# Two blocks' transposes moved from TensorE to DMA, and the visits of the second batch moved, in a sigmoid-attention and ReGLU kernel on Trainium2

## The chip, the cores and the metric

The kernel runs on one core of one Trainium2 chip. The metric is the device time of one execution in microseconds. Before the change it is 430.22 us, the median of three runs (430.01 to 430.52). The profile is of one execution, with a span of 428.4 us from the first instruction to the last.

## The reference

Sigmoid attention over 8 batches of 12 heads, 448 positions, 64 features a head, and then a ReGLU feed-forward layer on the 3584 tokens of 768 features, with a hidden width of 1536:

```python
scores = (1/sqrt(64)) * q @ k^T - log(448)
attn   = 1 / (1 + exp(-scores))
x      = (attn @ v), heads side by side            # 3584 x 768
out    = (max(x @ w_gate, 0) * (x @ w_val)) @ w_out
```

Inputs and output are in float32; the kernel multiplies in float16.

## The kernel before

The twelve heads of a batch form three blocks of four heads; block `n` has `b, i = divmod(n, 3)`, so that blocks 0 to 2 are batch 0, blocks 3 to 5 are batch 1, block 6 begins batch 2. A block has seven passes (chunks of 64 keys). Blocks 0 to 2 are worked off in a prologue. Then the loop over batches runs the feed-forward layer of batch `b` on TensorE and slips the attention of batch `b + 1` into it, in "visits" of three passes.

q and k must stand transposed, with the features on the partitions, before scores can be formed. There are two ways to that in the kernel. From block 6 on it is a DMA transpose on the SyncE queue; up to block 5 it is TensorE, with a copy out of PSUM:

```python
    def dma_transposes(n: int):
        for nm in ("k", "q"):
            h16 = qk16.pop((nm, n))
            t2 = qkTp.tile([P, NCH, 2, KC], FP16, tag="qkT", name=f"{nm}T")
            nc.sync.dma_start_transpose(
                t2[:].rearrange("p c h k -> p c (h k)"), h16[:].rearrange("p c r d -> p (c r d)")
            )
            qkT[nm, n] = t2

    def transposes(n: int, nm: str, *engines, cut=(0, NCH)):
        h16 = qk16.pop((nm, n))
        if n <= NBLK:
            tr = wkp.tile([P, NCH, 2, KC], FP16, tag="wk", name="tr")
        else:
            tr = qkp.tile([P, 2, 512], FP32, tag="qk", name="tr")[:, 0, 0 : S].bitcast(FP16)
            ...
        for c in range(cut[0], cut[-1]):
            nc.tensor.transpose(tr[:, c], h16[:, c, :, :], ident[:])
        ...                                   # one VectorE copy of tr into the qkT tile
```

The buffers that play a part: four tiles `qkT` (k and q of two blocks), four tiles `h16` (the float16 k and q before they are transposed), five staging tiles for weights, ten for q, k and v. PSUM has three tiles of two banks for scores, values and such (`qkp`) and two of one bank for the feed-forward layer (`wkp`).

A visit works off three passes; one of the two batch-1 blocks before may get its values (28 matmuls) in it. Each pass then calls `feed`:

```python
    def feed(i: int):
        n, c = divmod(i, NCH)
        m = n + 1
        if c == 0 and NPRO <= m < NB:          # NPRO is 6
            cast_block(m)
        if c == 4 and NBLK < m < NPRO:         # blocks 4 and 5
            later.append(m)
        if c == 3 and NPRO <= m < NB:
            dma_transposes(m)
        if c == 3 and NPRO <= m + 1 < NB:
            load_all(m + 1)
```

Weights and the inputs of blocks 3 to 5 are loaded in one order, one item at a time: ten items during the prologue, then one at every eighth step of the feed-forward layer. Each load is followed by its casts to float16 on GpSimd:

```python
        order = halves("g", 0) + ["kq"] + halves("u", 0) + ["v"] + halves("g", 1) + halves("u", 1)
        order += [4] + halves("g", 2) + halves("u", 2) + halves("o", 0) + [5]
        order += halves("o", 1) + halves("o", 2)

        def start_next():
            what = order.pop(0)
            if isinstance(what, int):
                load_all(what)                 # k, q, v of the block
                cast_block(what)               # q, k, v, on GpSimd
            ...
            else:
                load_w(*what)
                cast_w(*what, nc.gpsimd)
```

The loop, where a step is one matmul of a gate or value tile, or one of the down part:

```python
        for b in range(B):
            total = ffn_us(b)
            todo = []
            if b + 1 < B:
                count = NBLK * NCH // 3 + (1 if b == 0 else 0)
                lo = 6.0 if b == 0 else 0.0
                todo = [lo + (k + 0.5) * (total - lo) / count for k in range(count)]
            t = 0.0
            for step, cost in enumerate(ffn(b)):
                t += cost
                if order and step % 8 == 0:
                    start_next()
                if todo and t >= todo[0]:
                    due = todo.pop(0) + 2.0
                    visit()
                if later and t >= due:
                    m = later.pop(0)
                    transposes(m, "k")
                    transposes(m, "q")
```

`ffn(b)` takes the twelve gate and value tiles first (six matmuls for the gate, six for the value; the first pair of batch 0 is partly done before the loop) and then the down part with `wo`, in two column ranges of twelve matmuls for each 128 tokens. `total` is 38.88 in the kernel's own units for batch 0.

Of the kernel before, what the change touches and what calls it, by code (L numbers as in the profile page):

```python
# [16 lines left out]
def kernel(  # L17
# [16 lines left out]
    NBLK = H // HB  # L34
# [50 lines left out]
    def load_block(n: int, *which):  # L85
        b, i = divmod(n, NBLK)
        for nm, src, c0, c1, eng in which:
            st = stp.tile([P, 2, S], FP32, tag="st", name=f"st_{nm}")
            rows = src[b, i * HB : (i + 1) * HB].rearrange("(r h) (p c) d -> (h p) r (c d)", h=2, c=NCH)
            eng.dma_start(st[:, :, c0 * D : c1 * D], rows[:, :, c0 * D : c1 * D])  # L90
            staged[nm, n] = st

    def load_all(n: int, names="kqv"):
        for nm, src in (("k", k), ("q", q), ("v", v)):
            if nm in names:
                load_block(n, (nm, src, 0, NCH, nc.sync))

    def cast_qk(n: int, nm: str, *engines, cut=(0, NCH)):
        st = staged.pop((nm, n))
        h16 = h16p.tile([P, NCH, 2, D], FP16, tag="h16", name=f"h16{nm}")  # L100
        for c0, c1, eng in zip(cut, cut[1:], engines):
            o = h16[:, c0:c1].rearrange("p c r d -> p r c d")
            i = st[:, :, c0 * D : c1 * D].rearrange("p r (c d) -> p r c d", d=D)
            if eng is nc.scalar:
                eng.copy(o, i)
            else:
                eng.tensor_copy(o, i)  # L107
        qk16[nm, n] = h16

    def cast_v(n: int, eng):  # L110

        st = staged.pop(("v", n))
        t = v16p.tile([P, 2, S], FP16, tag="v16", name="v16")
        eng.tensor_copy(t[:, 0], st[:, 0])  # L114
        eng.tensor_copy(t[0:64, 1], st[64:128, 1])  # L115
        eng.tensor_copy(t[64:128, 1], st[0:64, 1])  # L116
        v16[n] = t

    def load_w(kind: str, j: int, half: int):

        st = swp.tile([P, WH], FP32, tag="sw", name=f"st_w{kind}")
        if kind == "o":
            r0 = (j * FG + half * FG // 2) * P
            src = moe_w_out[r0 : r0 + FG // 2 * P, :].rearrange("(c p) m -> p c m", p=P)
            nc.sync.dma_start(st[:].rearrange("p (c m) -> p c m", m=DM), src)
        else:
            w, r0 = moe_w_gate if kind == "g" else moe_w_val, half * NDC // 2 * P
            src = w[r0 : r0 + NDC // 2 * P, j * FG * P : (j + 1) * FG * P]
            nc.sync.dma_start(
                st[:].rearrange("p (c f) -> p c f", f=FG * P), src.rearrange("(c p) f -> p c f", p=P)  # L130
            )
        staged[kind, j, half] = st

    def cast_w(kind: str, j: int, half: int, eng):
        st = staged.pop((kind, j, half))
        dst = {"g": wg, "u": wv, "o": wo}[kind][j]
        n = (FG if kind == "o" else NDC) // 2
        dst = dst[:, half * n : (half + 1) * n].rearrange("p c f -> p (c f)")
        eng.tensor_copy(dst, st[:])  # L139
# [10 lines that stand above are left out]
# [165 lines left out]
    NPRO = 2 * NBLK  # L315

    def cast_block(n: int):
        cast_qk(n, "q", nc.gpsimd)
        cast_qk(n, "k", nc.gpsimd)
        cast_v(n, nc.gpsimd)  # L320

    def feed(i: int):

        n, c = divmod(i, NCH)
        m = n + 1
        if c == 0 and NPRO <= m < NB:
            cast_block(m)
        if c == 4 and NBLK < m < NPRO:
            later.append(m)
        if c == 3 and NPRO <= m < NB:  # L330
            dma_transposes(m)
        if c == 3 and NPRO <= m + 1 < NB:
            load_all(m + 1)
# [25 lines left out]
    def filler(*widths):  # L359

        if 0 not in PT:
            PT[0] = qkp.tile([P, 2, 512], FP32, tag="qk", name="pv_ps")
        for w in widths:
            nc.tensor.matmul(PT[0][:, 0, 0:w], zeros[:, 0:P], zeros[:, 0:w], start=True, stop=True)

    with tc.manual_schedule():
        nc.scalar.activation(warm[:], bias_t[:], AF.Sigmoid)  # L367

        sp, act = nc.sync, nc.scalar
        load_block(0, ("q", q, 0, NCH, sp), ("k", k, 0, 4, act), ("k2", k, 4, NCH, sp), ("v", v, 0, NCH, act))  # L370
        load_block(1, ("k", k, 0, NCH, sp), ("q", q, 0, NCH, act), ("v", v, 0, NCH, sp))
        load_block(2, ("k", k, 0, NCH, act), ("q", q, 0, NCH, sp), ("v", v, 0, NCH, sp))

        def halves(kind, j):
            return [(kind, j, 0), (kind, j, 1)]

        order = halves("g", 0) + ["kq"] + halves("u", 0) + ["v"] + halves("g", 1) + halves("u", 1)
        order += [4] + halves("g", 2) + halves("u", 2) + halves("o", 0) + [5]
        order += halves("o", 1) + halves("o", 2)

        def start_next():
            what = order.pop(0)
            if isinstance(what, int):
                load_all(what)
                cast_block(what)
            elif isinstance(what, str):
                load_all(NBLK, what)
                if what == "v":
                    cast_v(NBLK, nc.gpsimd)
# [4 lines that stand above are left out]
        filler(*[512] * 10)  # L394
        cast_qk(0, "q", nc.vector, nc.scalar, cut=(0, 4, NCH))
        cast_qk(0, "k", nc.vector, nc.scalar, cut=(0, 2, 4))
        transposes(0, "q")
        filler(128, 128)
        transposes(0, "k", nc.scalar, nc.vector, cut=(0, 2, 4))
        filler(128, 128, 128)  # L400
        cast_qk(0, "k2", nc.vector, cut=(4, NCH))
        for n in range(NBLK):
            cast_v(n, nc.gpsimd)
        for _ in range(2):
            start_next()


        NP0 = NBLK * NCH
        done = 0
        for i in range(NP0 + 2):  # L410
            n, c = divmod(i, NCH)
            if n < NBLK:
                scores(n, c)
            while done <= i - (4 if i < NP0 - 4 else 2):
                values(done // NCH, [done % NCH])
                done += 1
            if i == 2:
                qk16["k", 0] = qk16.pop(("k2", 0))
                transposes(0, "k", nc.vector, cut=(4, NCH))
            if 1 <= i <= 3:  # L420
                filler(256)
            if c == 1 and n + 1 < NBLK:
                cast_qk(n + 1, "k", nc.vector)
                cast_qk(n + 1, "q", nc.vector)
            if c in (3, 5) and n + 1 < NBLK:
                transposes(n + 1, "k" if c == 3 else "q")
            if i == 15:
                cast_qk(NBLK, "k", nc.vector)
            if i == 17:
                cast_qk(NBLK, "q", nc.vector)  # L430
                transposes(NBLK, "k")
            if i in (18, 21):
                gv_part(0, 0, wg, [0, 1] if i == 18 else [2, 3])
            if i == 20:
                transposes(NBLK, "q")
            if 11 <= i < NP0:
# [4 lines that stand above are left out]
            todo = []  # L441
            if b + 1 < B:
                count = NBLK * NCH // 3 + (1 if b == 0 else 0)
                lo = 6.0 if b == 0 else 0.0
                todo = [lo + (k + 0.5) * (total - lo) / count for k in range(count)]
            t = 0.0
            for step, cost in enumerate(ffn(b)):
# [10 lines that stand above are left out]
            for _ in todo:  # L458
                visit()
# [29 lines left out]
```

## Time and profile before

| | before |
|---|---|
| median time | 430.22 us |
| span of the profiled execution | 428.4 us |
| TensorE busy | 418.1 us, 98% |
| ScalarE, VectorE, GpSimd busy | 178.5, 166.5, 102.2 us |
| moved by DMA | 66.96 MB, 156 GB/s on average |
| TensorE transposes (`tr`) in the whole run | 84, of which 28 are blocks 4 and 5 |
| DMA transposes in the whole run | 36 |

In the page and the answers of the trace, a row names the line of the program, the engine, the operation, what it writes and what it reads. `gv_ps` are the gate and value tiles, `y_ps` the down part, `qk_ps` the scores, `pv_ps` the values, `tr` the TensorE transposes; `st_q`, `st_wo` and the like are staging tiles for loads, `h16k` and the like their float16 copies. PE is TensorE, DVE VectorE, ACT ScalarE, POOL GpSimd, SP SyncE. In a timeline or in the chain, the first number is the start in microseconds from the start of the span, the second the length; in brackets stands how long the engine sat idle before, and what ended that.

### The profile page before, as it was taken

To read this page: it belongs to the slowest core of one execution; us is meant where nothing else is said; L and a number is where in the kernel's file an instruction comes from. 1 tells how busy PE (TensorE), PEld (TensorE's weight loads), DVE (VectorE), ACT (ScalarE), POOL (GpSimd) and SP (SyncE) were. 2 spreads that over 40 slices of the span, in tenths; PEclk is the share of its full clock that TensorE was granted. 3 is DMA by queue.
4 is the path that set the end of the run, shared out by engine and by line. 5 is a ranking of instruction groups with operands and counts; after the bars stand their busy time and mean duration, and the time that the engine had idled before them with its cause. 6 is when DMAs were issued, how large, how long until landed. Compare 5 with 4: busy or idle time off the path is not lost.

```text
span 428.4 us, 7873 instructions
## 1 busy us (share of the span) xinstructions
PE 418.1 (98%) x3282; PEld 216.5 (51%) x3282; DVE 166.5 (39%) x276; ACT 178.5 (42%) x217; POOL 102.2 (24%) x137
## 2 busy tenths in 40 slices
PE   7789999999999999999999999999999999999996
PEld 4334555544555445545455444554455544555553
DVE  3555542353323452244423444244422435235531
ACT  5952566525434445444343545443435363500000
POOL 2567683333300333013120233003330030000000
PEclk9999999999999999999999999999999999999999
DMA  8999996673535753386623666247443730030014
GB/s 303 384 385 385 390 373 155 184 196 115 160 98 103 205 149 113 78 206 174 170 50 94 179 173 173 73 95 207 121 150 98 181 72 0 20 93 0 2 37 110
DMA packets 64371, 66.96 MB, mean 156 GB/s; under 512 B 35792, under 2 KB 54608, under 8 KB 64336
## 3 DMA queue, kind: packets, MB, share of 16 engines
q1 hardware_dynamic: 63088, 64.63, 51.8%
q10 hardware_dynamic: 1248, 1.84, 1.2%
q8 instruction: 25, 0.41, 0.4%
q14 instruction: 10, 0.08, 0.1%
HBM read 47.19 MB, written 11.01 MB: 136 GB/s over the span
## 4 chain that ended last, share of the span: by engine, by line
PE 93%; ACT 3%; DMA 2%; DVE 1%; issue 0%; ACTq 0%; DVEq 0%
PE gv_ps L232 51%; PE y_ps L275 26%; PE qk_ps L173 8%; PE pv_ps L197 7%; ACT PT L183 3%; DMA st_q<-in_q_dram 2%; PE tr L159 1%; DVE ysb L289 0%; DVE gate_sb L249 0%; DVE xT L213 0%; DVE h16q L107 0%; ACT L367 0%; ACT xT L211 0%; ACTq L295 0%; ACTq L90 0%
## 5 line engine op out<-in xcount | busy, mean ns | idle before, releaser
L183 ACT ACTIVATE PT<-qk_ps,bias_t 128x896 f16<-128x896 f32 x168 | 159.2, 1008 | 191.1 <-PE qk_ps L173 191.1
L232 PE MATMUL gv_ps<-xT,wg 128*128 128x448 f16 x576 | 128.1, 353 | 0.4 <-ACT xT L211 0.2
L232 PE MATMUL gv_ps<-xT,wv 128*128 128x448 f16 x576 | 126.9, 353 | 0.0
L275 PE MATMUL y_ps<-wo,hT 128*128 128x512 f16 (+2 forms) x684 | 113.7, 323 | 0.0
L275 PEld LDWEIGHTS <-hT 128*128 128x128 f16 x684 | 64.6, 98 | 48.0 <-issue 6.3
L249 DVE TENSOR_SCALAR gate_sb<-gv_ps 128x448 f32<-128x448 f32 x96 | 59.9, 624 | 73.4 <-PE gv_ps L232 73.4
L256 DVE TENSOR_TENSOR hT<-gate_sb,gv_ps 128x448 f16<-128x448 f32 x96 | 59.6, 621 | 64.3 <-PE gv_ps L232 64.2
L232 PEld LDWEIGHTS <-wg 128*128 128x128 f16 x576 | 55.0, 98 | 55.7 <-issue 7.7
L232 PEld LDWEIGHTS <-wv 128*128 128x128 f16 x576 | 55.0, 98 | 54.8 <-issue 5.2
L289 DVE TENSOR_SCALAR ysb<-y_ps 128x512 f32<-128x512 f32 (+2 forms) x56 | 31.1, 555 | 105.3 <-PE y_ps L275 104.1
L107 POOL CAST h16q<-st_q 128x896 f16<-128x896 f32 x20 | 18.6, 930 | 220.0 <-DMA st_q<-in_q_dram 195.3
L173 PE MATMUL qk_ps<-qT,kT 64*64 64x448 f16 x672 | 48.6, 358 | 3.9 <-ACT PT L183 2.9
L197 PE MATMUL pv_ps<-PT,v 64*64 64x448 f16 x672 | 39.1, 350 | 0.8 <-ACT PT L183 0.7
L173 PEld LDWEIGHTS <-kT 64*64 64x64 f16 x672 | 16.5, 105 | 29.8 <-issue 22.7
L197 PEld LDWEIGHTS <-v 64*64 64x64 f16 x672 | 19.9, 107 | 12.7 <-issue 2.1
L211 ACT ACTIVATE xT<-pv_ps 128x448 f16<-128x448 f32 x43 | 21.0, 547 | 6.0 <-PE pv_ps L197 4.8
L287 ACT ACTIVATE ysb<-y_ps 128x128 f32<-128x128 f32 x1 | 0.3, 277 | 44.8 <-PE y_ps L275 44.8
L107 POOL CAST h16k<-st_k 128x896 f16<-128x896 f32 x20 | 18.6, 928 | 0.0
L114 POOL CAST v<-st_v 128x448 f16<-128x448 f32 x24 | 13.3, 556 | 10.3 <-DMA st_v<-in_v_dram 10.3
L115 POOL CAST v<-st_v 64x448 f16<-64x448 f32 x24 | 13.4, 558 | 1.5
L116 POOL CAST v<-st_v 64x448 f16<-64x448 f32 x24 | 13.3, 555 | 1.0
L139 POOL CAST wv<-st_wu 128x1536 f16<-128x1536 f32 x6 | 8.8, 1467 | 5.7 <-DMA st_wu<-in_moe_w_val_dram 5.7
(26 smaller groups left out, 59.3 us busy)
## 6 DMA issues: line engine op xcount, KB each, us to landing
out_dram<-ysb SPq DMA_DIRECT2D x54, 192.0 KB, 2.7
st_q<-in_q_dram SPq DMA_DIRECT2D x23, 448.0 KB, 4.5
st_v<-in_v_dram SPq DMA_DIRECT2D x23, 448.0 KB, 5.2
st_k<-in_k_dram SPq DMA_DIRECT2D x22, 448.0 KB, 4.0
st_wg<-in_moe_w_gate_dram SPq DMA_DIRECT2D x6, 768.0 KB, 12.3
st_wu<-in_moe_w_val_dram SPq DMA_DIRECT2D x6, 768.0 KB, 12.2
st_wo<-in_moe_w_out_dram SPq DMA_DIRECT2D x6, 768.0 KB, 12.1
st_v<-in_v_dram ACTq DMA_DIRECT2D x1, 448.0 KB, 5.8
```

What stands on the lines that cost most here:

```text
L107: eng.tensor_copy(o, i)
L114: eng.tensor_copy(t[:, 0], st[:, 0])
L115: eng.tensor_copy(t[0:64, 1], st[64:128, 1])
L173: nc.tensor.matmul(ps[o : o + 64, bank, 0:S], kT[r : r + 64, c, h, :], qT[r : r + 64, :, h, :], start=True, stop=True, tile_position=(r, o ...
L183: nc.scalar.activation(pt[:], ps[:, :, 0:S], AF.Sigmoid, bias=bias_t[:], scale=qk_scale)
L197: nc.tensor.matmul(pv[o : o + 64, pr, 0:S], t[r : r + 64, pr, c * D : (c + 1) * D], pt[r : r + 64, pr, :], start=(c == 0), stop=(c == NCH ...
L211: nc.scalar.activation(x[:], pv[:, pr, 0:S], AF.Copy, scale=XSCALE)
L232: nc.tensor.matmul(begun[key][:, 0:S], w[j][:, dc, jj * P : (jj + 1) * P], xT[b, dc][:], start=(dc == 0), stop=(dc == NDC - 1),)
L249: nc.vector.tensor_scalar(out=g_sb[:], in0=gate[:, 0:S], scalar1=0.0, scalar2=None, op0=AOP.max)
L256: nc.vector.tensor_tensor(out=hT[f][:, o : o + S], in0=g_sb[:], in1=val[:, 0:S], op=AOP.mult)
L275: nc.tensor.matmul(y[:, 0:w], hT[f][:, o : o + P], wo[f // FG][:, f % FG, c0 : c0 + w], start=(f == 0), stop=(f == NFC - 1),)
L289: nc.vector.tensor_scalar(out=dst, in0=y[:, 0:w], scalar1=OUT_SCALE, scalar2=None, op0=AOP.mult)
```

## The change

Blocks 4 and 5 no longer go through TensorE. Their transposes are put into the load order as items of their own, `-4` behind the last gate and value weights and `-5` behind the last `wo`, and go to the SyncE queue as DMA transposes. The visits of batch 1 begin later in the feed-forward layer of batch 0 (`lo` is 10 in place of 6) and stand closer together, so that the transposes have time to come. The purpose is to free TensorE of 28 transposes and VectorE of four copies. The PSUM split and the matmuls on zeros ahead of the first tiles are as they were.

```diff
@@ feed
-        if c == 4 and NBLK < m < NPRO:
-            later.append(m)
@@ the load order
-        order += [4] + halves("g", 2) + halves("u", 2) + halves("o", 0) + [5]
-        order += halves("o", 1) + halves("o", 2)
+        order += [4] + halves("g", 2) + halves("u", 2) + [-4] + halves("o", 0) + [5]
+        order += halves("o", 1) + halves("o", 2) + [-5]
 
         def start_next():
             what = order.pop(0)
-            if isinstance(what, int):
+            if isinstance(what, int) and what < 0:
+                dma_transposes(-what)
+            elif isinstance(what, int):
                 load_all(what)
                 cast_block(what)
@@ the loop over batches
-                lo = 6.0 if b == 0 else 0.0
+                lo = 10.0 if b == 0 else 0.0
```

## The prediction

> **What bounds the kernel now.** I read the page's busy times first, then its chain of work, then the stretch of the chain that the change touches, and last the GpSimd timeline, which shows when the loads land.
>
> ```profile
> PE 418.1 (98%) x3282; PEld 216.5 (51%) x3282; DVE 166.5 (39%) x276; ACT 178.5 (42%) x217; POOL 102.2 (24%) x137
> ...
> PE 93%; ACT 3%; DMA 2%; DVE 1%; issue 0%; ACTq 0%; DVEq 0%
> ```
>
> TensorE is busy for 98% of the span and is 93% of the chain that ended last. Outside the first 30 us nothing else decides the end. So a matmul taken away inside the loop shortens the run by its own length, and a wait of TensorE there lengthens it by the whole wait. The chain between 43 and 66 us, in order of time (start, length, what):
>
> ```profile
> 42.96 0.69 PE qk_ps L173 x12
> 43.65 2.00 PE gv_ps L232 x10
> 45.65 0.78 PE tr L159 x14
> 46.43 2.30 PE gv_ps L232 x12
> 48.73 0.69 PE qk_ps L173 x12
> ...
> 57.71 0.78 PE tr L159 x14
> 58.49 2.08 PE gv_ps L232 x11
> 60.57 0.69 PE qk_ps L173 x12
> 61.26 1.43 PE gv_ps L232 x7
> 62.69 2.81 PE y_ps L275 x14
> ```
>
> The two rows `tr` are what the change removes, for block 4 and block 5. The `qk_ps` rows of 0.69 us are visits of batch 1 (three chunks of scores each). The rows follow one another without a hole: TensorE waits for nothing here.
>
> The other side is the DMA. In the windows from 28 to 60 us its share is 1.03 to 1.05 at 384 to 397 GB/s: the engines are full until the last weights and block 6 have come. The GpSimd timeline shows it as casts that each wait for a landing:
>
> ```profile
> 38.64 0.93 POOL L107 CAST h16k<-st_k 128x896 f16<-128x896 f32 x1
> ...
> 46.99 1.47 POOL L139 CAST wv<-st_wu 128x1536 f16<-128x1536 f32 x1 [0.56 <-DMA st_wu<-in_moe_w_val_dram]
> 49.28 1.47 POOL L139 CAST wo<-st_wo 128x1536 f16<-128x1536 f32 x1 [0.82 <-DMA st_wo<-in_moe_w_out_dram]
> 51.28 1.47 POOL L139 CAST wo<-st_wo 128x1536 f16<-128x1536 f32 x1 [0.54 <-DMA st_wo<-in_moe_w_out_dram]
> 53.75 0.93 POOL L107 CAST h16q<-st_q 128x896 f16<-128x896 f32 x1 [1.00 <-DMA st_q<-in_q_dram]
> 54.63 0.93 POOL L107 CAST h16k<-st_k 128x896 f16<-128x896 f32 x1
> ...
> 60.72 1.47 POOL L139 CAST wo<-st_wo 128x1536 f16<-128x1536 f32 x1 [0.50 <-DMA st_wo<-in_moe_w_out_dram]
> 62.72 1.47 POOL L139 CAST wo<-st_wo 128x1536 f16<-128x1536 f32 x1 [0.53 <-DMA st_wo<-in_moe_w_out_dram]
> ```
>
> To be seen: the last value weights land at 46.95, two halves of `wo` at 49.25 and 51.25, block 5's q at 53.6, the last half of `wo` at 62.7. Everything comes in the order in which SyncE issues it, 2.0 us for each half of a weight (768 KB).
>
> [...] This trace has 14 in 0.78 us on TensorE's chain (56 ns each, pipelined), and 3.0 us from issue to landing for one DMA transpose of seven tiles (a k or a q of a block). [...] the landings above agree, and so a transpose put behind a load waits for that load. [...] the first ten 512-column fillers took 4.45 us, 0.43 us each, against 14 of the down part in 2.81 us later (0.20 each; the row of the chain above), the full clock is recorded from 6.6 us, 5.4 us after the first matmul, and in the window from 426.5 us, after the last matmul, the clock reads 0.50.
>
> **The change, part by part.**
>
> Removed: two groups of 14 TensorE transposes, 2 x 0.78 = 1.56 us on the chain. Their four VectorE copies (0.62 us each) lie beside matmuls and are worth nothing. Gain 1.56 us, 0.36%.
>
> Moved: eight visits, the same work. I ran the loop's bookkeeping by hand (137 steps of 0.189 in the gate and value part, then the down part). Before, the visits fall on steps 42, 64, 86, 107, 129, ...; after, on 62, 81, 100, 119, 138, .... Step 138 is the second of the down part. Block 4 is first needed in the second pass of visit 2, block 5 in the third pass of visit 4 (24 passes from 21; block 5 begins with pass 35). A step is 0.189 us in the trace too (2.27 us for 12). So, from visit 0 at 37.93 us:
> - visit 0: 37.93 + 20 x 0.189 = 41.7
> - visit 1: + 19 x 0.189 + 0.79 (visit and its seams: 4.96 us measured between visits 0 and 1, less 22 x 0.189) = 46.1
> - visit 2: 50.5; block 4 needed at 50.7
> - visit 3: 54.9; with block 3's values, 2.1 us, and 17 steps, the down part starts at 60.2
> - visit 4: 60.6; block 5 needed at about 61.1.
>
> Added: four DMA transposes in SyncE's order, two behind the value weights, two behind all of `wo`. Each moves 229 KB as 896 packets of 256 bytes, which take 21 ns of an engine: 896 x 21 / 16 = 1.2 us in a full queue; in steady state two follow one another by 1.3 us. SyncE issues in order: block 4's wait for the cast that ends at 39.57, so they are in the ring long before the queue reaches them.
> - Block 4's land behind the last value weights: 46.95 + 1.25 + 1.25 = 49.4. Needed at 50.7: in time, by 1.3 us.
> - All of `wo` and block 5 shift by the 2.5 us that these take: block 5's cast ends at 55.56 + 2.5 = 58, the last `wo` lands at 62.7 + 2.5 = 65.2.
> - Block 5's sit behind it: 65.2 + 2.5 = 67.7; the q half lands at about 67.5 (67.0 to 68.5).
> - Needed at 61.1. TensorE, in order, stops inside visit 4 for **about 6.4 us**.
>
> A second, hidden wait lies below it: the down part now starts 2.3 us earlier (60.2 against 62.5, because a visit and the transposes went from before it), and its eleventh step needs the last `wo`, cast only at 65.2 + 1.5 = 66.7. Without block 5's wait it would still stop there for some 3.5 us (61.1 + 0.2 for the third pass and 8 more steps of 0.216, the distance of the 512-column matmuls in the timeline, give 63.1).
>
> Clock: 6.4 us of idle is enough for the clock to fall to half. [...] I take 2.2 us.
>
> Sum: 430.2 - 1.6 + 6.4 + 2.2 = 437.2; I say **437.0 us**, +1.6%. Nothing later gives it back: every later stretch is bound by TensorE. Block 6's loads are issued only after block 5's transposes (about 60.5 instead of 51.3), so that its own transposes land near 76 instead of 71.3; they are needed in visit 7, at 76.6 before and some 83 with the stall, so no third wait.
>
> **Rivals.**
> 1. *The transposes are hidden and the gain stays*: 428.7. For it: block 4's fits with 1.3 us to spare, and the trace's transposes land within 3.1 us when the queue is empty. Against it: the queue is full until 64 us, and block 5's stand behind four more weight loads. I give it 1 in 10.
> 2. *The weights of the down part become the wait* (block 5's transposes come earlier than I think, or overlap the weights): a stop of 3.5 us at the eleventh step of the down part, perhaps with no clock loss: 430.2 - 1.6 + 3.5 = 432 to 434. 2 in 10.
> 3. *Both blocks are late*: if the ring takes block 4's transposes only when the weights before them have drained, or a packet of them costs more beside loads, visit 2 stops too, by 1 to 2 us, and everything behind moves: 438 to 441. 2 in 10.
> 4. *VectorE's freed copies speed TensorE up*: no row of the chain between 43 and 66 us waits for VectorE, so nothing.
>
> **Range and chances.** The stall can be 5 to 8 us, [...] the gain is sure. This gives 432 to 440 for 8 in 10. Slower by over 2% needs 438.8 or more, another 1.8 us on top of the sum: 0.21. Faster by over 2% would need five times the removed work: 0.01. The rest, 0.78, is within 2%.
>
> **What would show it.** Right: the chain has no `tr` after 30 us; TensorE has one hole, inside the fifth visit, ended by the DMA transpose of q (or k) of block 5, from about 61 to 67.5; the last cast of `wo` starts near 65; the clock dips to 0.5 near 65 to 70 and matmuls there take twice as long; past 75 us every row of the chain has the length it had. Wrong: no hole (rival 1), a hole that starts in the down part and ends with a cast of `wo` (rival 2), a hole near 51 (rival 3), or a hole without a dip of the clock, which would take 2 us off.

## The result, and the profile after

The changed kernel takes 437.14 us, the median of four runs (436.05 to 437.4), against 430.12 us for the kernel before beside it (430.01 to 430.52). The ratio is 1.0157, with a 95% interval of 1.0138 to 1.0176: 7.0 us, or 1.6%, longer.

The busy times and the shares of the chain, from the page of the kernel after:

```profile
PE 419.1 (96%) x3254; PEld 215.6 (50%) x3254; DVE 163.3 (37%) x272; ACT 178.6 (41%) x217; POOL 103.0 (24%) x137
...
PE 91%; DMA 4%; ACT 3%; DVE 1%; issue 0%; ACTq 0%; DVEq 0%
```

TensorE has 28 matmuls fewer, and yet 1 us more of busy time, because some of them ran at half the clock, as shown below; its share fell, and a DMA took a part of the chain that it didn't have. The chain in order of time (start, length, what) says which:

```profile
51.30 0.69 PE qk_ps L173 x12
51.99 3.70 PE gv_ps L232 x19
55.69 0.50 PE qk_ps L173 x8
56.19 1.32 PE pv_ps L197 x28
57.52 0.19 PE qk_ps L173 x4
57.70 3.06 PE gv_ps L232 x16
60.77 6.38 DMA qT<-h16q
67.14 0.14 issue
67.28 0.59 PE qk_ps L173 x4
67.87 5.80 PE y_ps L275 x23
```

No `tr` is left. Visit 2 at 51.30 goes through: block 4 was there. In visit 4 the DMA transpose of block 5's q holds everything until 67.14; the 6.38 us of its row run from its issue to its landing, and TensorE waits through the later part of them. TensorE's row in the timeline of the same stretch gives the idle time before it in brackets:

```profile
67.28 0.59 PE L173 MATMUL qk_ps<-qT,kT 64*64 64x448 f16 x4 [5.32 <-DMA qT<-h16q]
```

The last row of the chain is the second loss: 23 matmuls of the down part in 5.80 us, 0.25 each, with the faster ones at its end. The windows around the hole (stretch, its length, then busy time and number of instructions of PE, PEld, DVE, ACT and POOL), with TensorE's granted clock, as a share of the full one, as the third figure from the end:

```profile
63.00:65.00 2.00, 0.00 (x0) 0.00 (x0) 0.00 (x0) 0.79 (x1) 1.51 (x2) 1.00 1.34 295
67.20:71.90 4.70, 4.62 (x14) 1.67 (x15) 0.00 (x0) 1.01 (x1) 2.18 (x3) 0.50 0.69 244
71.90:75.00 3.10, 3.10 (x46) 2.07 (x48) 1.11 (x2) 0.90 (x1) 1.25 (x3) 1.00 0.00 0
```

The clock is at half from 65.08 to 71.91 us. Of that, TensorE works from 67.28 on: 4.63 us at half speed, a loss of 2.3 us.

The landings, as the GpSimd casts show them, and the issues of the DMA transposes on SyncE (the second figure is how long SyncE was occupied):

```profile
39.62 1.33 SPq L146 DMA_TRANSPOSE kT<-h16k  x1
41.01 5.24 SPq L146 DMA_TRANSPOSE qT<-h16q  x1
...
51.88 1.47 POOL L139 CAST wo<-st_wo 128x1536 f16<-128x1536 f32 x1 [3.34 <-DMA st_wo<-in_moe_w_out_dram]
...
65.60 1.47 POOL L139 CAST wo<-st_wo 128x1536 f16<-128x1536 f32 x1 [0.50 <-DMA st_wo<-in_moe_w_out_dram]
```

The first half of `wo` is cast at 51.88 where it was 49.28, the last at 65.60 where it was 62.72: 2.6 and 2.9 us later. The 2.6 us are the price of block 4's two transposes in front of them; the other 0.3 us comes in behind block 5's loads, and what makes it is not shown.

The books close. Before, the first gate of batch 1 began at 79.27 us in the timeline, now at 86.13, and the last matmul moved by the same 6.86 us (424.21 to 431.07). At equal work, the third pass of visit 4 would have come at 62.7 in the kernel before (60.90, and 7 steps of 0.19 and 2 of 0.216 for the work that now stands ahead of it); it came at 67.28. That is 4.6 us, which holds both the 1.56 us saved and the wait, and the clock's 2.3 us make it 6.9. Everything after is unchanged. TensorE came to the loop 0.7 us late in this execution (its first full gate tile starts at 31.38 instead of 30.65, in a part that the change doesn't touch); the hole swallowed that, because its end is set by the DMA.

### The profile page after: what moved, and what is told of

Read it like the earlier page. It is cut to its first block, busy times and chain, and to the rows that moved or that the text cites. A ratio compares the mean times of both kernels' runs of the same rounds, so it can differ in the third digit from the quotient of the medians.

```text
span 435.5 us, 7815 instructions
## 1 busy us (share of the span) xinstructions
PE 419.1 (96%) x3254; PEld 215.6 (50%) x3254; DVE 163.3 (37%) x272; ACT 178.6 (41%) x217; POOL 103.0 (24%) x137
## 3 DMA queue, kind: packets, MB, share of 16 engines
q1 hardware_dynamic: 66800, 65.55, 53.6%
## 4 chain that ended last, share of the span: by engine, by line
PE 91%; DMA 4%; ACT 3%; DVE 1%; issue 0%; ACTq 0%; DVEq 0%
PE gv_ps L232 51%; PE y_ps L275 26%; PE qk_ps L173 8%; PE pv_ps L197 7%; ACT PT L183 2%; DMA st_q<-in_q_dram 2%; DMA qT<-h16q 1%; DVE ysb L289 0%; PE tr L159 0%; DVE xT L213 0%; DVE gate_sb L249 0%; DVE h16q L107 0%; ACT L365 0%; ACT xT L211 0%; ACTq L295 0%
## 5 line engine op out<-in xcount | busy, mean ns | idle before, releaser
L275 PE MATMUL y_ps<-wo,hT 128*128 128x512 f16 (+2 forms) x684 | 115.8, 327 | 0.0
L173 PEld LDWEIGHTS <-kT 64*64 64x64 f16 x672 | 16.5, 105 | 36.0 <-issue 22.5
```

The costliest lines, as they stand in the source:

```text
L173: nc.tensor.matmul(ps[o : o + 64, bank, 0:S], kT[r : r + 64, c, h, :], qT[r : r + 64, :, h, :], start=True, stop=True, tile_position=(r, o ...
L275: nc.tensor.matmul(y[:, 0:w], hT[f][:, o : o + P], wo[f // FG][:, f % FG, c0 : c0 + w], start=(f == 0), stop=(f == NFC - 1),)
```

## Experiments

The theory: block 5's transposes stand at the end of a full queue, TensorE waits for them in order, and the idle time costs clock on top. The rivals: moving the visits costs the time; a DMA transpose is slow beside loads wherever it stands; the casts of `wo` are the real wait. All times are medians, with the ratio to the kernel before on the same chip in brackets; the kernel before has 429.8 to 429.9 us in them.

**e1: block 5 back on TensorE, block 4 by DMA.**

```diff
-        order += halves("o", 1) + halves("o", 2) + [-5]
+        order += halves("o", 1) + halves("o", 2)
+        if c == 4 and m == NBLK + 2:
+            later.append(m)
```

> Block 4 by DMA, block 5 back on TensorE, visits as in the changed kernel. Queue theory (block 5's transposes stand behind all of wo and land at 67.1 us, 5.4 us after they are needed, and the clock then costs 2.3): the hole in visit 4 and the clock loss go, but the last wo still lands 2.5 us later than before, behind block 4's transposes, so the down part stops for 2 to 3 us for casts of wo: about 432 us (430.1 - 0.8 + 2.6), no dip of the clock. Visits theory (moving the visits later costs the 7 us by itself): stays at 436 to 437. Transposes theory (a DMA transpose beside loads is slow for everything): half of the loss stays, about 434.

Measured: 434.82 us (1.0114, 1.0099 to 1.0129). TensorE's waits in its timeline:

```profile
64.65 0.59 PE L275 MATMUL y_ps<-wo,hT 128*128 128x512 f16 x2 [1.35 <-POOL wo L139]
67.46 3.74 PE L275 MATMUL y_ps<-wo,hT 128*128 128x512 f16 x15 [2.21 <-POOL wo L139]
```

The hole in visit 4 is gone and the hidden wait stands in the open: 3.6 us for the two last casts of `wo`. But my 432 missed by nearly 3 us: about one of them is that wait, longer than the 2.6 I had put down; the other 1.7 is a dip of the clock to half from 67.76 to 71.17 that I had ruled out. Waits of 1.35 and 2.21 us, with two matmuls between them, were enough for it. The saving of 0.78, the waits and the dip sum to 4.5 us; the stretch up to batch 1 took 4.7 longer.

**e2: the later visits alone**, with all transposes of the kernel before.

```diff
-                lo = 6.0 if b == 0 else 0.0
+                lo = 10.0 if b == 0 else 0.0
```

> The kernel before with nothing but the later visits (lo 10). Queue theory: all work before the eleventh step of the down part is the same, the last wo is cast at 64.2 and needed at 64.7, so no wait: 430.1 us (429.7 to 430.7). Visits theory: 436 to 437.

Measured: 430.01 us (1.0005, 0.9995 to 1.0015). The move by itself costs nothing that can be measured.

**e3: TensorE kept busy through the wait**, with matmuls on zeros whose result nobody reads.

```diff
+            if i == 5 * NCH:
+                idle = qkp.tile([P, 2, 512], FP32, tag="qk", name="idle_ps")
+                for _ in range(23):
+                    nc.tensor.matmul(idle[:, 0, :], zeros[:, 0:P], zeros[:], start=True, stop=True)
             scores(*divmod(i, NCH))
```

> The changed kernel with 23 matmuls of 512 columns on zeros (5.0 us of work that is thrown away) right before the pass that waits for block 5. Queue theory: the wait ends at the same 67.1 us, the clock stays at 1.00, and the 4.6 us that ran at half speed after the wait run at full speed: 437.1 - 2.3 = 434.8 us. Rival (the clock's dip costs nothing because that stretch waits for the casts of wo anyway): 437 us.

Measured: 435.26 us (1.0138, 1.0108 to 1.0168). The wait's end, and the window after it:

```profile
67.58 0.38 PE L173 MATMUL qk_ps<-qT,kT 64*64 64x448 f16 x4 [1.64 <-DMA qT<-h16q]
```

```profile
67.60:72.00 4.40, 4.40 (x35) 2.51 (x39) 1.12 (x2) 1.01 (x1) 2.00 (x3) 1.00 0.69 247
```

The wait ends where it did (67.58 against 67.28), the clock stays at 1.00, and 35 matmuls (some of them narrower) run in 4.4 us where 14 ran in 4.7 in the changed kernel. From the end of the wait to the first gate of batch 1 it is 16.6 us (67.58 to 84.21) instead of 18.9 (67.28 to 86.13): the dip's price is 2.2 us. It was not hidden beside anything. The time is 1.9 us under the 437.14 of the changed kernel (1.7 when each is set against the kernel before beside it); the wait ended 0.3 us later here. Three of the four executions took 435.1 to 435.4 us; the fourth took 437.92, at a mean granted clock of 0.994, and has no profile.

**e4: visits later still** (`lo` 14), so that visit 4 comes after the tenth step of the down part.

```diff
-                lo = 10.0 if b == 0 else 0.0
+                lo = 14.0 if b == 0 else 0.0
```

> The changed kernel with lo 14 in place of 10: visit 4 falls after the tenth step of the down part instead of the second. Queue theory with the hidden wait on wo: TensorE now stops first at the ninth step of the down part for the third quarter of the wo casts (about 2.5 us), then in visit 4 for block 5 (about 1.4 us), in sum 3.8 us, [...]: 430.4 - 1.6 + 3.8 = 432.6 us. If only block 5 made a wait: about 430. If later visits are bad in themselves: over 437.

Measured: 435.59 us (1.0126, 1.0109 to 1.0143). Its waits:

```profile
61.21 0.59 PE L275 MATMUL y_ps<-wo,hT 128*128 128x512 f16 x2 [0.47 <-POOL wo L139]
62.62 0.59 PE L275 MATMUL y_ps<-wo,hT 128*128 128x512 f16 x2 [0.82 <-POOL wo L139]
64.55 0.59 PE L275 MATMUL y_ps<-wo,hT 128*128 128x512 f16 x2 [1.34 <-POOL wo L139]
66.69 0.59 PE L173 MATMUL qk_ps<-qT,kT 64*64 64x448 f16 x4 [1.05 <-ACT PT L183]
```

```profile
66.00:72.70 6.70, 6.01 (x23) 3.03 (x24) 1.12 (x2) 2.39 (x3) 3.93 (x6) 0.50 0.61 212
```

As expected the one hole fell apart into waits for `wo` and one in visit 4, 3.7 us in sum (3.8 expected). The row of visit 4 names a ScalarE instruction, which ended at 66.57; block 5's q landed at 66.56, so the trace can't tell which of the two TensorE waited for. The expected sum had no loss of clock in it, but the clock fell, from 65.96 to 72.79 us: 6.0 us of work at half speed, 3.0 us lost. That is the miss between 432.6 and 435.6.

**e5: visits where they were** (`lo` 6), both blocks by DMA.

```diff
-                lo = 10.0 if b == 0 else 0.0
+                lo = 6.0 if b == 0 else 0.0
```

> The changed kernel with the visits where they were before (lo 6). Queue theory: the landings stay (block 4 at 50.0, block 5 at 67.1 us), the needs move forward, so visit 2 stops for about 1.5 us and visit 4 for about 6.0 us, and the clock costs 2.3: 430.4 - 1.6 + 1.5 + 6.0 + 2.3 = 438.7 us. Visits theory (the move costs the time): 429.

Measured: 439.68 us (1.0229, 1.0209 to 1.0249).

```profile
49.93 0.57 PE L173 MATMUL qk_ps<-qT,kT 64*64 64x448 f16 x8 [2.00 <-DMA qT<-h16q]
67.85 0.59 PE L173 MATMUL qk_ps<-qT,kT 64*64 64x448 f16 x4 [4.80 <-DMA qT<-h16q]
```

```profile
50.70:54.10 3.40, 3.40 (x11) 1.40 (x10) 1.24 (x2) 1.63 (x2) 1.81 (x2) 0.50 1.03 396
...
67.80:71.10 3.30, 3.25 (x12) 1.35 (x13) 0.62 (x1) 1.01 (x1) 0.81 (x1) 0.50 0.96 344
```

Both blocks are late, and each hole brings its own dip of the clock, 1.7 us each: 3.4 us where I had put down 2.3 for one, which is the miss between 438.7 and 439.7. So the later visits were the helpful half of the change: without them it would be 2.5 us slower still (2.9 when each is set against the kernel before on its own chip).

**e6: the queue ahead of block 5 made shorter.** The v loads of blocks 4 and 5 go behind its transposes; values need them only later.

```diff
-        order += [4] + halves("g", 2) + halves("u", 2) + [-4] + halves("o", 0) + [5]
-        order += halves("o", 1) + halves("o", 2) + [-5]
+        order += [("L", 4, "kq")] + halves("g", 2) + halves("u", 2) + [-4] + halves("o", 0) + [("L", 5, "kq")]
+        order += halves("o", 1) + halves("o", 2) + [-5, ("L", 4, "v"), ("L", 5, "v")]
         ...                                   # start_next loads and casts what an "L" item names
```

> The changed kernel with the v loads of blocks 4 and 5 (1.17 us of the full queue each) put behind block 5's transposes; v is needed only when a block's values are formed. Queue theory: block 5's transposes land 2.35 us earlier, at 64.8, the hole in visit 4 shrinks from 5.4 to 3.1 us; 432.0 us if the clock stays up, 434.2 if it still falls. A theory in which block 5's transposes are late because of their own cost or their cast, and not of the queue before them: unchanged, 437.

Measured: 434.72 us (1.0105, 1.0084 to 1.0126).

```profile
64.86 0.59 PE L173 MATMUL qk_ps<-qT,kT 64*64 64x448 f16 x4 [3.96 <-DMA qT<-h16q]
```

Two loads of 1.17 us taken away from ahead of it, and the wait ends 2.4 us earlier (64.86 against 67.28). The landing is set by the place in the queue, and not by the cast: the transposes were issued only 0.9 us earlier (57.26 against 58.19). The hole is 4.0 and not 3.1 us long because TensorE came to it 1.1 us earlier in this execution (60.90 against 61.96), and the clock fell (63.69 to 70.52).

**e7: v loads last and visits later** (e6 with `lo` 14).

```diff
-                lo = 10.0 if b == 0 else 0.0
+                lo = 14.0 if b == 0 else 0.0
```

> Both: v loads last and lo 14. Queue theory: the third quarter of wo is cast at 62.7, when the down part needs it, block 5 lands at 64.8 and is needed at 63.5: one hole of about 1.4 us, no dip of the clock: 430.2 us.

Measured: 431.08 us (1.0030, 1.0021 to 1.0039), 0.9 us over the expectation. In the profiled execution, which took 432.71:

```profile
62.28 0.59 PE L275 MATMUL y_ps<-wo,hT 128*128 128x512 f16 x2 [0.43 <-POOL wo L139]
65.04 0.59 PE L173 MATMUL qk_ps<-qT,kT 64*64 64x448 f16 x4 [1.66 <-DMA qT<-h16q]
```

```profile
64.80:68.10 3.30, 3.06 (x15) 1.67 (x16) 0.69 (x1) 1.41 (x2) 1.86 (x5) 0.50 1.05 377
```

The waits are 2.1 us, and here the clock dipped for 3.41 us. Fourteen of the sixteen executions took 430.6 to 431.6 us and two 432.7. Both of the two have a mean granted clock of 0.995, and twelve of the fourteen have 0.998 or more (the other two, at 431.4 and 431.6 us, have 0.994). A dip that comes in some executions only would make that step of 1.7 us; only one of them has a profile, so this stays an inference.

**e8: v loads last, and the first tile of the down part worked off in both column ranges before the last rows of `wo` are touched**, with visit 4 after twenty of its steps (`lo` 16.5).

```diff
+        for f0, f1 in ((0, 10), (10, NFC)):
+            for m0, mn in ranges:
+                ...                            # the matmuls of rows f0 to f1 of this range
-            yield from down(col0)
+            yield from (down_first() if col0 == 0 else down(col0))
         ...                                   # order as in e6; lo = 16.5
```

> v loads last, visit 4 after twenty steps of the down part (lo 16.5), and the first 128 tokens of the down part worked off in both column ranges up to the tenth of twelve rows of wo before the last two rows are touched, which moves the need of the last wo by 1.1 us. Queue theory: wo cast at 64.7 and needed at 64.1 to 64.6, block 5 at 64.8 and needed at 64.6: holes of under 0.5 us in sum, so nearly the whole 1.6 us of removed transposes is gained: 429.0 us (428.5 to 429.7), under the kernel before. If the clock or the queue has another wait in store (block 6's transposes land near 76 and are needed near 76): 430 to 432.

Measured: 431.98 us (1.0048, 1.0032 to 1.0065): the expectation failed.

```profile
62.89 1.68 PE L307 MATMUL y_ps<-wo,hT 128*128 128x512 f16 x12 [0.94 <-POOL wo L139]
65.53 0.38 PE L173 MATMUL qk_ps<-qT,kT 64*64 64x448 f16 x4 [0.45 <-DMA qT<-h16q]
67.23 2.32 PE L275 MATMUL y_ps<-wo,hT 128*128 128x512 f16 x10 [0.56 <-DVE ysb L317]
```

Small waits took the place of the large one: for `wo`, for block 5, and for the two PSUM banks, which both end at the same moment in this order and wait for VectorE. A further one comes at the end of the stage. The chain there, in order of time:

```profile
79.46 0.75 ACT PT L183
80.21 0.14 issue
80.35 0.98 ACT xT L211 x2
81.34 0.04 issue
81.38 2.43 PE gv_ps L232 x12
```

The visits, pushed together, leave ScalarE at work when batch 1 wants to begin: from its first gate tile to the next value tile it is 1.49 us (80.08 to 81.57), against 1.13 in the kernel before (79.27 to 80.40). So `lo` can't be raised at will: a part of what is freed ahead of the weights is paid on ScalarE at the end.

**e9: only block 5 by DMA**, block 4 on TensorE, v loads last, `lo` 12.

```diff
+        if c == 4 and m == NBLK + 1:
+            later.append(m)
-        order += [4] + halves("g", 2) + halves("u", 2) + [-4] + halves("o", 0) + [5]
-        order += halves("o", 1) + halves("o", 2) + [-5]
+        order += [("L", 4, "kq")] + halves("g", 2) + halves("u", 2) + halves("o", 0) + [("L", 5, "kq")]
+        order += halves("o", 1) + halves("o", 2) + [-5, ("L", 4, "v"), ("L", 5, "v")]
         ...                                   # lo = 12.0
```

> Block 4 on TensorE as before, only block 5 by DMA, v loads of both blocks behind its transposes, lo 12 (visit 4 after the fifth or sixth step of the down part). Queue theory: nothing new stands ahead of wo, and two v loads less, so the last wo is cast near 62.4 (needed at 63.9) and block 5 lands near 62.4 to 62.9 (needed near 62.1 to 62.5): holes of 0.5 us at the most, no dip of the clock, half of the removed transposes gained: 429.2 us (428.8 to 429.8) against 429.9. If a DMA transpose in this stretch costs the run something by itself: 431 or more.

Measured: 430.54 us (1.0019, 1.0012 to 1.0025): slower than the kernel before, not faster, so the expectation failed.

```profile
52.38 0.38 PE L173 MATMUL qk_ps<-qT,kT 64*64 64x448 f16 x4
52.82 0.62 DVE L165 COPY kT<-tr 128x896 f16<-128x896 f16 x1 [1.81 <-PE qk_ps L173]
...
54.03 0.57 PE L173 MATMUL qk_ps<-qT,kT 64*64 64x448 f16 x8 [1.26 <-DVE qT L165]
```

The waits near 62 us are gone, and one has come at 52: block 4's copies out of PSUM wait for a score of block 3. With the DMA transposes of block 5 ahead of them in the program, block 5 took the free `qkT` buffers and block 4 was left with those of block 3. This version made that wait itself (e11 takes it away), and it is a wait on a buffer that no share of busy time shows.

**e10: v loads last alone**, in the kernel before.

```diff
-        order += [4] + halves("g", 2) + halves("u", 2) + halves("o", 0) + [5]
-        order += halves("o", 1) + halves("o", 2)
+        order += [("L", 4, "kq")] + halves("g", 2) + halves("u", 2) + halves("o", 0) + [("L", 5, "kq")]
+        order += halves("o", 1) + halves("o", 2) + [("L", 4, "v"), ("L", 5, "v")]
```

> The kernel before with the v loads of blocks 4 and 5 behind wo and nothing else. Queue theory: TensorE had no hole to fill, so the same as before: 429.9 us (429.6 to 430.3). If the order of the loads is worth something by itself, it shows here.

Measured: 429.89 us (1.0001, 0.9993 to 1.0009): nothing, as expected.

**e11: e9 with block 4's TensorE transposes ahead of block 5's in the order**, `lo` 13.

```diff
-        if c == 4 and m == NBLK + 1:
-            later.append(m)
-        order += halves("o", 1) + halves("o", 2) + [-5, ("L", 4, "v"), ("L", 5, "v")]
+        order += [("o", 1, 0), -4, ("o", 1, 1)] + halves("o", 2) + [-5, ("L", 4, "v"), ("L", 5, "v")]
-                dma_transposes(-what)
+                if what == -4:
+                    transposes(4, "k")
+                    transposes(4, "q")
+                else:
+                    dma_transposes(-what)
```

> As the run with block 5 alone by DMA, but block 4's TensorE transposes stand in the load order ahead of block 5's DMA transposes, so that block 4 gets the free qkT buffers and its copies do not wait for block 3's last scores; visit 4 after the eighth step of the down part (lo 13). Queue theory with the buffer order as the cause of the 1.35 us hole: no hole over 0.3 us, no dip of the clock, 0.78 us gained: 429.2 us (428.8 to 429.5). If the hole had another cause it stays: 430.5.

**e12: e11 with block 5 on TensorE too**, as its control.

```diff
-        order += [("o", 1, 0), -4, ("o", 1, 1)] + halves("o", 2) + [-5, ("L", 4, "v"), ("L", 5, "v")]
+        order += [("o", 1, 0), -4, ("o", 1, 1)] + halves("o", 2) + [("L", 4, "v"), ("L", 5, "v")]
+        if c == 4 and m == NBLK + 2:
+            later.append(m)
```

> The same with block 5 on TensorE too (no DMA transpose of blocks 4 and 5; v loads last, lo 13): no hole and no gain, 429.9 us (429.6 to 430.3). The difference to the run with block 5 by DMA is then the price of 14 TensorE transposes, 0.78 us.

Measured: e11 429.57 us (0.9993, 0.9985 to 1.0001), e12 429.81 us (1.0000, 0.9991 to 1.0008). In e11 TensorE has no hole. Its chain where the wait was:

```profile
61.04 1.73 PE y_ps L275 x8
62.77 0.69 PE qk_ps L173 x12
63.46 3.36 PE y_ps L275 x21
```

From the first full gate tile to the first gate of batch 1 it took 47.84 us in the timeline (30.58 to 78.42), 48.62 in the kernel before (30.65 to 79.27) and 48.62 in e12 (29.89 to 78.51): the 0.78 us of 14 transposes are gained there to the digit. In the whole run's time 0.2 to 0.3 us of it are seen, and the interval holds 1. So the expectation for e11 (428.8 to 429.5) was just missed: it is faster in this stretch, but not shown to be faster in time. In the profiled executions two things hide the gain. Behind the stretch 0.1 us is lost in the first tiles of batch 1 (1.25 us from the first gate tile to the value tile, against 1.13), and ahead of it the start of the loop differs from one execution to the next by as much as the gain: the first full gate tile is at 29.89 us in e12 and at 30.58 in e11, and both profiled executions have a span of 427.8 us.

## Why the prediction was right

The time was 437.14 against 437.0, and the terms hold one by one:

- **Block 4 in time**: yes. Landed by 50.0 us by the trace's semaphores (49.4 predicted), needed at 51.4 (50.7 predicted). The margin is partly luck, because TensorE was 0.7 us late here: in e1 and e3, with the same order and visits, the q of block 4 landed at 49.85 and 50.17 and was needed at 50.39 and 50.35, a margin of 0.5 and 0.2 us. So rival 3 was nearer than the predicted margin of 1.3 us makes it look.
- **Block 5 behind all of `wo`**: landed at 67.14 (67.5 predicted), inside visit 4. e6 shows that it is the place in the queue: 2.35 us of loads less, 2.4 us earlier. e2 rules out the moved visits as the cause, and e10 that the order of the v loads is worth something by itself. The transposes themselves were not slow beside loads: block 5's k and q landed 0.8 and 1.6 us behind the last `wo` (65.55, 66.35 and 67.14).
- **The stall of 6.4 us**: 5.3 in the profile. TensorE was 0.7 us late when it came to it, and the landing was 0.35 earlier; the first of these is without effect on the end. At equal work, saving and wait together came to 4.6 us; the prediction had -1.6 + 6.4 = 4.8.
- **The hidden wait on `wo`**: shown in e1 and e4. With block 5 out of the way 3.6 us of it remain, as I had put it (some 3.5).
- **The clock, 2.2 us**, my estimate: 2.3 in the profile, 2.2 by the profile of e3, 1.7 to 1.9 in its time.
- **Rivals**: 1 (hidden, 428.7) fell, 2 is true as the next wait in line, 3 didn't come in the changed kernel but did in e5. 4 was not tested by itself; no row of the chain shown waits for VectorE.

What was wrong in it: sizes that partly cancel, so that the total is nearer than its terms. Block 4's pair cost the loads behind it 2.6 to 2.9 us and not 2.5, and block 5's pair landed 1.6 us after the last `wo` and not 2.5. Block 6's loads were issued at 64.1 us and not at 60.5, and its transposes landed at 79.6 and not near 76; they were needed at 83.7, so there was no third wait, as predicted. The low end of the range doesn't follow from its terms: a stall of 5 us with no loss of clock gives 433.6, not 432. And the reading of rival 2, "perhaps with no clock loss": e1 and e4 show that waits in pieces cost clock as well. Had the change been e1 or e4, the same working would have been 3 us too low; my expectations of those two were.

## What to carry to other kernels

To move work from the busiest engine to a DMA queue pays only as early as the queue can deliver: put the time of landing (everything ahead of it in the queue, at the measured rate; in e6, 2.35 us of loads less ahead of it brought it 2.4 us earlier) beside the time of need, for the item moved and for all that it pushes back. A stall of TensorE can cost more than its length, because the clock may fall with it; e3 priced that at 2.2 us for one hole, and the next section says after which waits it fell here. And a wait taken away uncovers the next one: here block 5, `wo`, the PSUM banks, ScalarE and a buffer's order stood one behind the other, for a gain that was 1.56 us at best.

## What was not expected of the hardware

- **The clock fell after shorter waits than I thought.** One wait of 2.00 us was enough (e5, at 49.93), and 1.35 and 2.21 us with two matmuls between (e1), and 0.43 and 1.66 us with ten between (e7); after 1.64 us (e3) and the three waits of e8, 0.94, 0.45 and 0.56 us, the clock stayed at 1.00. The longest wait alone doesn't decide it: in e4 the clock fell at 65.96 after waits of 0.47, 0.82 and 1.34 us, at the beginning of a fourth. What decides it is not shown. The mean granted clock from 60 to 75 us was 0.77 in the changed kernel, e4 and e6, 0.89 in e1, e5 and e7, and 1.00 in e3 and e8: at half the full clock, dips of 6.83 us in the first three and of 3.41 us in the next three (e5 had one more, from 50.7). The dip lasted 3.41 us where TensorE waited for at most 0.33 us of it (e1, e5, e7), and 6.83 us where it waited for 0.73 us or more (e4, e6, the changed kernel).
- **A DMA transpose held SyncE for long in a full queue**: block 4's q held it for 5.24 us and block 5's k and q for 2.48 and 3.28, although block 4's k took 1.33; of the 36 in the kernel before, 34 took 1.2 to 1.3. The loads of `wo` behind block 4's pair were issued from 46.3 us on instead of 36.8. From 48 to 49 and from 49 to 50 us the DMA share then fell to 0.65 and 0.86, where it was 1.01 and 1.05 in the kernel before: the queue was no longer full. By these four shares some 0.5 us of the 2.6 that the pair cost would be that gap, an estimate; it wasn't tested by itself.
